# A gMLP block with one bf16 gelu per row tile, in-place batched norms, and outputs three tiles behind the gates

## The chip, the cores and the metric

The kernel runs on one core of a Trainium2 chip. The metric is device time in microseconds (us), from one launch of the whole program; a median over several executions is given, and one execution was recorded by the hardware profiler.

The engines go by these names: PE is TensorE's matmul stream and PEld its weight loads, DVE is VectorE, ACT is ScalarE, POOL is GpSimd, SP is SyncE, which here only issues DMAs. Each engine runs its own instructions in program order, and engines wait for each other by semaphores.

## The reference, cut to what matters

Rows are S = 2048 tokens of 512 features. The model alternates two mixers, twice:

```
x = x + A(layernorm(x))      # attention over segments of 32 rows with 8 memory rows, 32 heads of 128
x = x + B(layernorm(x))      # gMLP
x = x + A(layernorm(x))
x = x + B(layernorm(x))
```

Only B is changed. It is, with Fh = 688:

```
z  = gelu_tanh(x @ w_in)                       # 2048 x 1376
z1 = z[:, :688]
z2 = layernorm(z[:, 688:])                     # over the 688 features
g  = w_sp @ z2 + b_sp[:, None]                 # w_sp is 2048 x 2048: it mixes the rows
B  = (z1 * g) @ w_out                          # 688 x 512
```

Inputs and the output are bf16; x is kept in f32 in between. The layer norms have no learned scale or shift.

## The kernel before, in words

The program is a chain of four stages, A, B, A, B. In time the first B stage lies at about 781 to 939 us of the span and the second at 1697 us to the end. `a_block` (L479) is the attention; `b_block` (L227) is the gMLP and takes all of the change but two lines.

**Row tiles.** The 2048 rows are 16 tiles of 128 (NT = 16). Three arrays in device memory carry rows from stage to stage: `xd` holds x in f32, `xb_d` the normalised rows in bf16 for B, `xn_d` those for A. `o_d` holds the attention's output before x is added to it.

**Order.** Inside `b_block` the instructions of PE, DVE, ACT and SP are issued in the order in which the program text makes them (`manual_schedule`). Those of POOL are placed by a scheduler. A tile of a pool of n buffers waits for the last reader of the tile n before it; when a pool is closed, its memory goes to later pools, whose first writers wait for the last users.

**Projection half.** For each row tile `project` (L261) makes 12 matmuls (L266) into one of two PSUM tiles `big` of three banks each: tile tt + 2 can't start before ACT has emptied tile tt. The columns of w_in are swapped when they are loaded, so columns 0 to 687 of the PSUM tile are the z2 part. ACT empties it with two gelus: L268 writes the z2 part in f32 to a small tile (four buffers), L269 the z1 part in bf16 to the persistent array `z1`. DVE then takes the statistics of the f32 z2 (two bn_stats, L273 and L274, one aggregate, L275). After every second tile `norms` (L277) works out 1/sqrt(var + eps) for the pair on DVE, by a bit trick and three Newton steps (`_rstd_dve`, L119, 12 small operations), and one more operation for the shift `nb` = -mean * rstd (L285). `normalise` (L289) on ACT scales and shifts a tile into the persistent bf16 array `z2n`; it is called two tiles after the pair's statistics, so that it stands behind the gelus of the next pair in ACT's order. Transposed loads bring the normalised input rows (`front.load_rows`, on SP's queue).

**Late rows.** Four of the 16 row tiles (12 to 15) have their attention output so late that A's end doesn't add x to it. `late_load` (L253) issues the loads of x and o (L207, L208) and the add on POOL (L213), which stores x back to `xd` (L214); The calls of `norms` after tiles 5 and 7 are given two late rows each: they take the rows' statistics on DVE, and `y_norm` (L219) normalises the rows on DVE (L223) and stores them to `xb_d` on POOL's queue, from where `load_rows` reads them for the last tiles. The third and fourth late row borrow buffers of other pools, one of them a buffer of the w_sp pool.

**Gate half.** `gate(t)` makes 32 matmuls (L332) for an output row tile t: 16 source tiles `st`, each in two column halves of 344, into a PSUM tile taken from the same two `big` buffers. The weights are a transposed tile of w_sp, loaded by `load_wsp` (L257) on SP's queue into one of three buffers. `product(t)` (L335) first issues the load of w_sp tile t + 3, then forms u = (g + b_sp) * z1 on DVE (L340) in one of two u buffers, whose last 80 columns are zero, and a transposing DMA on SP's queue makes `uT`. `load_x` fetches the residual rows on ACT's queue. `finish(t)` (L357) makes six matmuls (L360), five over 128 features and one over the last 48 (`FCH`), adds x on DVE and stores the row tile on ACT's queue; in block one it also takes the statistics for the next A, with the square root by two ACT functions, and for tiles 0 and 1 normalises the rows for A's start. finish(t - 2) stands inside gate(t), after source tile 9. At the start gates 0 and 1 run through source tiles 0 to 13 first, then 14 and 15. The last tile is turned by PE (`turn_u`, L349) and copied by two ACT copies (L354, L355) in place of a DMA.

**FILL_AHEAD.** In A each segment's matmul instructions are padded, by splitting a few matmuls in two, so that a segment takes three pages of 256 PE instructions; `FILL_AHEAD` (L29, read in `pads_of`, L671) says how far the first segment of each A stage is off. The count depends on how many PE instructions come before.

Of the kernel before, what the change touches and what calls it, by code (L numbers as in the profile page):

```python
# [8 lines left out]
F32 = mybir.dt.float32  # L9
# [19 lines left out]
FILL_AHEAD = ((0, 0, 0, 106), (0, 0, 0, 94))  # L29
FCH = [(0, 128), (128, 128), (256, 128), (384, 128), (512, 128), (640, 48)]  # L30
# [137 lines left out]
class _Rows:  # L168
# [33 lines left out]
    def y_load(self, tb, first, eng, x=None, o=None):  # L202
# [5 lines left out]
        eng.dma_start(o, self.o_d[M + tb * P:M + (tb + 1) * P, :])  # L208
        self.y[tb] = (o, x)

# [8 lines left out]
    def y_norm(self, tb, mean, rstd, store):  # L219

        o, _ = self.y.pop(tb)
        xn = self.pool.tile([P, DM], BF16, name="ln_xn", bufs=2)
        self.nc.vector.tensor_scalar(out=_nat(xn[:]), in0=_perm(o), scalar1=mean, scalar2=rstd, op0=ALU.subtract, op1=ALU.mult)  # L223
        store.dma_start(self.xb_d[tb * P:(tb + 1) * P, :], xn[:])


def b_block(tc, c, rows, front, xd, MV_out, RS_out, w_sp, w_out, S, first, out_final=None):  # L227
# [4 lines left out]
    with ExitStack() as ctx:  # L232
# [5 lines left out]
        ps_pool = ctx.enter_context(tc.tile_pool(name="b_ps", bufs=1, space=PSUM))  # L238
        big = _Tagged(ps_pool, "big", 2)
        one = _Tagged(ps_pool, "one", 2)  # L240
# [3 lines left out]
        z1 = mid.tile([P, NT, FH], BF16, name="z1")  # L244
        z2n = mid.tile([P, NT, FH], BF16, name="z2n")
        w_out_sb = mid.tile([P, 6, DM], BF16, name="w_out_sb")
        xt, z2, wsp, mv, rs, nb = {}, {}, {}, {}, {}, {}
# [5 lines left out]
        def late_load(tb, x=None, o=None):  # L253
            rows.y_load(tb, first, nc.gpsimd, x=x, o=o)
            rows.y_add(tb, first, nc.gpsimd, nc.gpsimd)

        def load_wsp(t):  # L257
            wsp[t] = wsp_pool.tile([P, NT, P], BF16, name="wspT", tag="wspT")
            nc.sync.dma_start_transpose(out=wsp[t][:], in_=w_sp[t * P:(t + 1) * P, :].rearrange("t (st s) -> t st s", s=P))

        def project(tt):  # L261
# [5 lines left out]
            z2[tt] = zp.tile([P, FH], F32, name="z2", bufs=4)  # L267
            nc.scalar.activation(out=z2[tt][:], in_=pz[:, 0:FH], func=ACT.Gelu_apprx_tanh)  # L268
            nc.scalar.activation(out=z1[:, tt, :], in_=pz[:, FH:FF], func=ACT.Gelu_apprx_tanh)  # L269
            if tt % 2 == 0:  # L270
                mv[tt // 2] = zp.tile([P, 4, 2], F32, name="mv")
            st = zp.tile([P, 2, nc.vector.BN_STATS_DIM], F32, name="bnst2")
            nc.vector.bn_stats(out=st[:, 0, :], in_=z2[tt][:, 0:344])  # L273
            nc.vector.bn_stats(out=st[:, 1, :], in_=z2[tt][:, 344:FH])  # L274
            nc.vector.bn_aggr(out=mv[tt // 2][:, tt % 2, :], in_=st[:])  # L275

        def norms(q, late):  # L277

            n = 4 if late else 2
# [647 lines left out]
```

The softmax here doesn't subtract the row's maximum and nothing guards it: scores larger than these inputs give would overflow.

## Time and profile before

| | before |
|---|---|
| median of 8 runs | 1847.6 us (1842.64 to 1859.84) |
| the profiled execution | 1854.23 us |
| its span | 1852.5 us |
| PE busy | 1751.1 us, 95% of the span |
| PEld busy | 1246.1 us, 67% |
| DVE busy | 1155.2 us, 62% |
| ACT busy | 1111.2 us, 60% |
| POOL busy | 136.9 us, 7% |
| mean granted TensorE clock | 0.991 |

By stage, in the same execution (busy us in each stretch):

| stretch of the span | length | PE | DVE | ACT | POOL | clock | DMA share |
|---|---|---|---|---|---|---|---|
| first A | 781.0 | 734.1 | 508.5 | 515.9 | 57.0 | 0.99 | 0.19 |
| B one, projection half | 47.3 | 38.5 | 37.6 | 32.6 | 15.0 | 1.00 | 0.61 |
| B one, gate half | 110.7 | 102.8 | 44.7 | 14.4 | 11.9 | 0.97 | 0.80 |
| second A | 758.0 | 736.5 | 495.8 | 510.8 | 37.6 | 0.99 | 0.16 |
| B two, projection half | 46.1 | 37.8 | 37.4 | 31.8 | 15.1 | 1.00 | 0.66 |
| B two, gate half | 109.4 | 101.4 | 31.1 | 5.7 | 0.3 | 0.98 | 0.67 |

How to read it: busy time counts an engine's own instructions; DMA issues and waits don't count as busy. Matmuls are pipelined and their ends are modelled, so a busy PE is not PE at its peak. The clock is the share of full TensorE speed that the chip granted. The DMA share is the mean busy share of the core's 16 DMA engines. The lines "A <- B" in a view of waits say that A's engine stood idle until B's instruction or DMA had finished.

The chain of work that ended last is PE for 86% of the span, DVE 4, DMA 4, issue 2, ACT 2, POOL 1. Of that, the gate matmuls (L332) are 7%, the output matmuls (L360) 3%, the projection's (L266) 1% of the span and the transposed u tiles 1%; most of the rest is attention.

### The profile page before, as it was taken

The page shows a single profiled execution, that of the slowest core. Times are in us where ns is not written, and L with a number is a line of the kernel's source. Part 1 is how long each engine was busy: PE and PEld are TensorE (multiplying, and loading weights), DVE is VectorE, ACT ScalarE, POOL GpSimd, SP SyncE. Part 2 cuts the span into 40 slices and gives each one's busy share as a digit, 9 for nine tenths or more (in the row PEclk, how much of TensorE's full clock was granted, in tenths as well). Part 3 has the DMA queues.
Part 4 walks back from the last instruction along what each step waited for, and adds up shares of the span by engine and source line. Part 5 has one row for each costly group of instructions (what it writes and reads, how often), then busy time and mean ns, then how long its engine had stood idle before and what let it go on. Part 6 is the DMA issues. An engine that isn't in the chain of part 4 may idle for free.

```text
span 1852.5 us, 109472 instructions
## 1 busy us (share of the span) xinstructions
PE 1751.1 (95%) x51176; PEld 1246.1 (67%) x51176; DVE 1155.2 (62%) x2700; ACT 1111.2 (60%) x2074; POOL 136.9 (7%) x289
## 2 busy tenths in 40 slices
PE   2999999999999999889989999999999999998798
PEld 1777777777777777645557777777777777775455
DVE  1666666677667766583346666666766676665722
ACT  1677777776667776471047667666776676665500
POOL 5000000000000000122010000000000000002000
PEclk8999999999999999999989999999999999999999
DMA  9100000021002111359830000001200120124585
GB/s 348 53 20 19 22 20 20 20 82 31 19 20 84 37 30 42 92 140 201 185 120 22 23 23 24 22 22 43 82 26 22 50 83 26 35 62 144 119 174 131
DMA packets 189327, 126.78 MB, mean 68 GB/s; under 512 B 135896, under 2 KB 164328, under 8 KB 188872
## 3 DMA queue, kind: packets, MB, share of 16 engines
q1 hardware_dynamic: 167016, 71.01, 16.4%
q0 software_dynamic: 10560, 34.07, 5.6%
q10 hardware_dynamic: 11296, 14.70, 2.6%
q8 instruction: 400, 6.55, 1.5%
q14 instruction: 55, 0.45, 0.1%
HBM read 59.29 MB, written 33.56 MB: 50 GB/s over the span
## 4 chain that ended last, share of the span: by engine, by line
PE 86%; DVE 4%; DMA 4%; issue 2%; ACT 2%; POOL 1%; SPq 0%; ACTq 0%; POOLq 0%; DVEq 0%
PE psm L544 24%; PE psV L544 13%; PE pw L599 12%; PE psb L544 10%; PE pg L332 7%; PE psS L722 5%; PE psO L745 4%; PE pwB L611 3%; PE py L360 3%; PE psD L797 2%; PE psM L787 1%; DMA uT<-u 1%; PE pz L266 1%; DMA Wo_sb<-in_A_Wo_dram 1%; PE psM L788 1%
## 5 line engine op out<-in xcount | busy, mean ns | idle before, releaser
L544 PEld LDWEIGHTS <-hA 128*32 128x32 bf16 x19868 | 541.8, 96 | 168.7 <-DVE hA L655 51.5
L701 ACT CAST rows<-psm 128x512 bf16<-128x512 f32 x512 | 300.1, 586 | 200.0 <-PE psm L544 200.0
L544 PE MATMUL psm<-Wq_sb,hA 128*32 128x256 bf16 (+1 forms) x5768 | 275.9, 319 | 10.9 <-DVE hA L655 9.5
L599 PE MATMUL pw<-Wo_sb,uT 128*32 128x128 bf16 x16640 | 264.3, 220 | 17.3 <-DVE uT L807 9.3
L599 PEld LDWEIGHTS <-uT 128*32 128x32 bf16 x16640 | 236.7, 97 | 63.6 <-DVE uT L807 50.5
L544 PE MATMUL psm<-Wk_sb,hA 128*32 128x256 bf16 (+1 forms) x6623 | 276.4, 298 | 1.8 <-issue 1.0
L544 PE MATMUL psV<-Wv_sb,hA 128*32 128x256 bf16 x7477 | 274.1, 284 | 0.9 <-issue 0.9
L705 DVE STREAM_TRANSPOSE QQ<-rows 128x512 bf16<-128x512 bf16 x256 | 182.0, 711 | 78.3 <-ACT rows L701 77.2
L726 ACT ACTIVATE E<-psS 128x448 bf16<-128x448 f32 x256 | 140.0, 547 | 121.6 <-PE psS L722 121.6
L757 DVE TENSOR_TENSOR uT<-psO,Rt 128x384 bf16<-128x384 f32 x256 | 138.6, 541 | 119.2 <-ACT Rt L813 118.9
L705 DVE STREAM_TRANSPOSE KA<-rows 128x512 bf16<-128x512 bf16 x256 | 181.8, 710 | 44.5 <-ACT rows L701 44.3
L807 DVE TENSOR_TENSOR uT<-psO,Rm 128x128 bf16<-128x128 f32 x256 | 62.6, 287 | 167.7 <-PE psD L797 167.7
L813 ACT ACTIVATE Rt<-Rt 128x512 f32<-128x512 f32 x256 | 157.4, 629 | 4.1
L332 PE MATMUL pg<-z2n,wspT 128*128 128x344 bf16 x1024 | 155.6, 310 | 1.0 <-DVE u L340 1.0
L332 PEld LDWEIGHTS <-wspT 128*128 128x128 bf16 x1024 | 98.2, 98 | 55.0 <-issue 8.2
L805 ACT ACTIVATE Rt<-psD 128x1024 f32<-128x1024 f32 x128 | 131.2, 1025 | 6.0
L544 PEld LDWEIGHTS <-hB 128*32 128x32 bf16 x3072 | 88.1, 97 | 68.0 <-DVE hB L559 24.9
L722 PEld LDWEIGHTS <-KA 128*64 128x64 bf16 x2048 | 79.8, 113 | 67.1 <-DVE KA L705 40.2
L729 DVE TENSOR_TENSOR E<-E,maskN 128x448 bf16<-128x448 bf16 x256 | 95.3, 372 | 45.4 <-ACT E L726 45.4
L544 PE MATMUL psb<-Wq_sb,hB 128*32 128x512 bf16 x1024 | 91.6, 389 | 25.9 <-DVE hB L559 25.9
L782 ACT CAST VA<-psV 128x512 bf16<-128x512 f32 x128 | 75.0, 586 | 61.9 <-PE psV L544 61.9
L722 PE MATMUL psS<-QQ,KA 128*64 128x80 bf16 x2048 | 110.1, 208 | 1.9 <-issue 1.0
(147 smaller groups left out, 2219.3 us busy)
## 6 DMA issues: line engine op xcount, KB each, us to landing
Wo_sb<-in_A_Wo_dram POOLq DMA_DIRECT2D x8, 1024.0 KB, 13.2
xs<-xd ACTq DMA_DIRECT2D x32, 256.0 KB
o_d<-o_sb SPq DMA_DIRECT2D x126, 64.0 KB
y_o<-o_d SPq DMA_DIRECT2D x24, 256.0 KB
xd<-y_o SPq DMA_DIRECT2D x22, 256.0 KB
Wq_sb<-in_A_Wq_dram POOLq DMA_DIRECT2D x8, 512.0 KB, 6.9
Wk_sb<-in_A_Wk_dram POOLq DMA_DIRECT2D x8, 512.0 KB, 10.9
Wv_sb<-in_A_Wv_dram POOLq DMA_DIRECT2D x8, 512.0 KB, 11.4
```

The lines of the kernel that those rows point to most:

```text
L332: nc.tensor.matmul(pg[t][:, k, 0:344], lhsT=wsp[t][:, st, :], rhs=z2n[:, st, 344 * k:344 * k + 344], start=(st == 0), stop=(st == NT - 1))
L544: nc.tensor.matmul(o, lhsT=lhs(kt, cg), rhs=r, start=(kt == 0 and a == 0), stop=(kt == KT - 1 or halved > 0), tile_position=(0, 32 * cg), ...
L599: nc.tensor.matmul(po[32 * cg:32 * cg + 32, 0:128], lhsT=lhs[:, n, :], rhs=wo_rhs(h, cg), start=(h == 0), stop=(h == H - 1), tile_position ...
L701: nc.scalar.copy(r[:], ps[:])
L705: nc.vector.transpose(out=QQ[:, j % 2, :, 0:32] if j < 2 else KA[:, j % 2], in_=r[:])
L722: nc.tensor.matmul(pS[64 * g:64 * g + 64, i, c0:80 if K is KA else 112], lhsT=K[:, r, n:n + 2, :].rearrange("p h k -> p (h k)"), rhs=q if ...
L726: nc.scalar.activation(out=E[:, r], in_=pS, func=ACT.Exp, scale=scale)
L729: nc.vector.tensor_tensor(out=E[:, r], in0=E[:, r], in1=maskN[:, j4, :].unsqueeze(1).to_broadcast([P, 4, 112]), op=ALU.mult)
L757: nc.vector.tensor_tensor(out=hview(uT_nxt[:], r, 8, 32), in0=oview(r, 8, 32), in1=Rr[:, :, :, 0:24], op=ALU.mult)
L782: nc.scalar.copy(VA[:, 1].rearrange("p i e -> p (i e)"), psV[1][:, 0, :])
L805: nc.scalar.activation(out=Rt[:], in_=psD[:], func=ACT.Ln)
L813: nc.scalar.activation(out=rt, in_=rt, func=ACT.Exp, scale=-1.0)
```

## The change

Nearly all of it lies in `b_block`; what is computed stays the same, but for roundings.

- **One z tile, one gelu.** `z1` and `z2n` become the two halves of one bf16 array `z` (16 x 1376 columns per partition), and one gelu over 1376 columns writes it. The f32 z2 tiles go, and the statistics are taken from the bf16 values.
- **Norms in place, in four batches.** The scalars are worked out for groups instead of pairs: row tiles 0 to 3 with two late rows, 4 to 6 with the other two, 7 to 11, and 12 to 15. `normalise` overwrites z2 in `z`; on ACT, after the gelus as the loop says, and for the last four tiles on DVE.
- **Late rows.** All eight loads are issued first, each x and then (by the function that `y_load` now returns) its o, in the order of the four late rows; then a memset and the loads of w_out, which came before them. The adds move from POOL to DVE (`late_sum`), after tile 3 and after tile 5, and the normalising moves from DVE to ACT (`late_norm`).
- **w_sp loads** start after tiles 2, 4 and 11 (7, 9 and 11 before).
- **PSUM.** The projection keeps two tiles of three banks, in a pool that ends with it; the gates get three tiles of two banks.
- **Padded last rows.** w_out's sixth block is zeroed first, so that all six output matmuls and all six transposes are over 128 rows and one ACT copy replaces two. `FCH` goes.
- **Three tiles behind.** uT gets three buffers, gates 0 and 1 stop first at source tile 11, gate 2 runs whole, and finish(t - 3) stands inside gate(t). After the last gate come finish(13), the turn of tile 15, finish(14), finish(15). `load_x(t - 1)` stands in `product(t)`, behind the transpose.
- **FILL_AHEAD** of the second A: 94 becomes 86.

A's own use of `y_load` calls the returned function at once. In the diff, `NT - 4 + k` is the late row's tile. The core of the diff:

```diff
-FILL_AHEAD = ((0, 0, 0, 106), (0, 0, 0, 94))
-FCH = [(0, 128), (128, 128), (256, 128), (384, 128), (512, 128), (640, 48)]
+FILL_AHEAD = ((0, 0, 0, 106), (0, 0, 0, 86))
...
-        eng.dma_start(o, self.o_d[M + tb * P:M + (tb + 1) * P, :])
         self.y[tb] = (o, x)
+        return lambda: eng.dma_start(o, self.o_d[M + tb * P:M + (tb + 1) * P, :])
...
-    def y_norm(self, tb, mean, rstd, store):
+    def y_norm(self, tb, mean, rstd, store, shift=None):
 
         o, _ = self.y.pop(tb)
         xn = self.pool.tile([P, DM], BF16, name="ln_xn", bufs=2)
-        self.nc.vector.tensor_scalar(out=_nat(xn[:]), in0=_perm(o), scalar1=mean, scalar2=rstd, op0=ALU.subtract, op1=ALU.mult)
+        if shift is not None:
+            self.nc.scalar.activation(out=_nat(xn[:]), in_=_perm(o), func=ACT.Identity, bias=shift, scale=rstd)
+        else:
+            self.nc.vector.tensor_scalar(out=_nat(xn[:]), in0=_perm(o), scalar1=mean, scalar2=rstd, op0=ALU.subtract, op1=ALU.mult)
         store.dma_start(self.xb_d[tb * P:(tb + 1) * P, :], xn[:])
...
-        ps_pool = ctx.enter_context(tc.tile_pool(name="b_ps", bufs=1, space=PSUM))
-        big = _Tagged(ps_pool, "big", 2)
-        one = _Tagged(ps_pool, "one", 2)
+        big = _Tagged(zctx.enter_context(tc.tile_pool(name="b_psz", bufs=1, space=PSUM)), "big", 2)
...
-        z1 = mid.tile([P, NT, FH], BF16, name="z1")
-        z2n = mid.tile([P, NT, FH], BF16, name="z2n")
+        z = mid.tile([P, NT, FF], BF16, name="z")
+        z2n, z1 = z[:, :, 0:FH], z[:, :, FH:FF]
...
-        def late_load(tb, x=None, o=None):
-            rows.y_load(tb, first, nc.gpsimd, x=x, o=o)
-            rows.y_add(tb, first, nc.gpsimd, nc.gpsimd)
...
-            z2[tt] = zp.tile([P, FH], F32, name="z2", bufs=4)
-            nc.scalar.activation(out=z2[tt][:], in_=pz[:, 0:FH], func=ACT.Gelu_apprx_tanh)
-            nc.scalar.activation(out=z1[:, tt, :], in_=pz[:, FH:FF], func=ACT.Gelu_apprx_tanh)
-            if tt % 2 == 0:
-                mv[tt // 2] = zp.tile([P, 4, 2], F32, name="mv")
+            nc.scalar.activation(out=z[:, tt, :], in_=pz[:, 0:FF], func=ACT.Gelu_apprx_tanh)
             st = zp.tile([P, 2, nc.vector.BN_STATS_DIM], F32, name="bnst2")
-            nc.vector.bn_stats(out=st[:, 0, :], in_=z2[tt][:, 0:344])
-            nc.vector.bn_stats(out=st[:, 1, :], in_=z2[tt][:, 344:FH])
-            nc.vector.bn_aggr(out=mv[tt // 2][:, tt % 2, :], in_=st[:])
-
-        def norms(q, late):
-
-            n = 4 if late else 2
-            for k, tb in enumerate(late):
-                rows.y_stats(tb, mv[q][:, 2 + k, :])
-            rs[q] = zp.tile([P, 4], F32, name="rs")
-            nb[q] = zp.tile([P, 2], F32, name="nb")
-            _rstd_dve(nc, zp, rs[q][:, 0:n], mv[q][:, 0:n, 1], n)
-            nc.vector.scalar_tensor_tensor(out=nb[q][:], in0=mv[q][:, 0:2, 0], scalar=-1.0, in1=rs[q][:, 0:2], op0=ALU.mult, op1=ALU.mult)
-            for k, tb in enumerate(late):
-                rows.y_norm(tb, mv[q][:, 2 + k, 0:1], rs[q][:, 2 + k:3 + k], nc.gpsimd)
-
-        def normalise(tt):
-            nc.scalar.activation(out=z2n[:, tt, :], in_=z2.pop(tt)[:], func=ACT.Identity, bias=nb[tt // 2][:, tt % 2:tt % 2 + 1],
-                                 scale=rs[tt // 2][:, tt % 2:tt % 2 + 1])
-
+            for k in range(2):
+                nc.vector.bn_stats(out=st[:, k, :], in_=z[:, tt, 344 * k:344 * k + 344])
+            nc.vector.bn_aggr(out=slot(tt), in_=st[:])
+
+        def slot(tt):
+            group = next(g for g in GROUPS if tt in g)
+            if group not in where:
+                where[group] = (zp.tile([P, 8, 2], F32, name="mv"), zp.tile([P, 8], F32, name="rs"), zp.tile([P, 8], F32, name="nb"))
+            return where[group][0][:, group.index(tt), :]
+
+        def norms(group):
+
+            mv, rs, nb = where[group]
+            n = len(group)
+            _rstd_dve(nc, zp, rs[:, 0:n], mv[:, 0:n, 1], n)
+            nc.vector.scalar_tensor_tensor(out=nb[:, 0:n], in0=mv[:, 0:n, 0], scalar=-1.0, in1=rs[:, 0:n], op0=ALU.mult, op1=ALU.mult)
+
+        def scalars(tt):
+            group = next(g for g in GROUPS if tt in g)
+            k = group.index(tt)
+            mv, rs, nb = where[group]
+            return mv[:, k, 0:1], rs[:, k:k + 1], nb[:, k:k + 1]
+
+        def normalise(*tts, dve=False):
+            for tt in tts:
+                mean, rstd, shift = scalars(tt)
+                if dve:
+                    nc.vector.tensor_scalar(out=z2n[:, tt, :], in0=z2n[:, tt, :], scalar1=mean, scalar2=rstd, op0=ALU.subtract, op1=ALU.mult)
+                else:
+                    nc.scalar.activation(out=z2n[:, tt, :], in_=z2n[:, tt, :], func=ACT.Identity, bias=shift, scale=rstd)
+
+        def late_sum(k):
+            rows.y_add(NT - 4 + k, first, nc.vector, nc.gpsimd)
+            rows.y_stats(NT - 4 + k, slot(("row", k)))
+
+        def late_norm(k):
+            mean, rstd, shift = scalars(("row", k))
+            rows.y_norm(NT - 4 + k, mean, rstd, nc.gpsimd, shift=shift)
+
+        GROUPS = ((0, 1, 2, 3, ("row", 0), ("row", 1)), (4, 5, 6, ("row", 2), ("row", 3)), (7, 8, 9, 10, 11), (12, 13, 14, 15))
+        wl = wsp_pool.tile([P, 2, DM], F32, name="wspL", tag="wspT")
+        places = ((None, None), (gp.tile([P, DM], F32, name="xs", bufs=3)[:], gp.tile([P, DM], F32, name="xo", bufs=1)[:]),
+                  tuple(gp.tile([P, DM], F32, name="xs", bufs=3)[:] for _ in range(2)), (wl[:, 0, :], wl[:, 1, :]))
+        for load in [rows.y_load(NT - 4 + k, first, nc.gpsimd, *places[k]) for k in range(4)]:
+            load()
+        nc.gpsimd.memset(w_out_sb[:, 5, :], 0.0)
         nc.gpsimd.dma_start(w_out_sb[:, 0:5, :], w_out[0:640, :].rearrange("(fc p) d -> p fc d", p=P))
         nc.gpsimd.dma_start(w_out_sb[0:48, 5, :], w_out[640:688, :])
-        late_load(NT - 4)
-        late_load(NT - 3, gp.tile([P, DM], F32, name="xs", bufs=3)[:], gp.tile([P, DM], F32, name="xo", bufs=1)[:])
-        late_load(NT - 2, *(gp.tile([P, DM], F32, name="xs", bufs=3)[:] for _ in range(2)))
-        wl = wsp_pool.tile([P, 2, DM], F32, name="wspL", tag="wspT")
-        late_load(NT - 1, wl[:, 0, :], wl[:, 1, :])
         for tt in range(NT):
             project(tt)
-            if tt in (7, 9, 11):
-                load_wsp((tt - 7) // 2)
-            if tt == 14:
-                load_x(0)
-            if tt % 2 == 1:
-                if tt // 2 + 3 < NT // 2:
-                    front.load_rows(tt // 2 + 3)
-                norms(tt // 2, {5: (NT - 4, NT - 3), 7: (NT - 2, NT - 1)}.get(tt, ()))
-                if tt > 1:
-                    normalise(tt - 3)
-                    normalise(tt - 2)
-        normalise(NT - 2)
-        normalise(NT - 1)
+            if tt % 2 == 1 and tt // 2 + 3 < NT // 2:
+                front.load_rows(tt // 2 + 3)
+            if tt in (2, 4, 11):
+                load_wsp((2, 4, 11).index(tt))
+            if tt == 3:
+                late_sum(0)
+                late_sum(1)
+                norms(GROUPS[0])
+                late_norm(0)
+                late_norm(1)
+                normalise(0)
+            elif tt == 4:
+                normalise(1)
+            elif tt == 5:
+                late_sum(2)
+                late_sum(3)
+                normalise(2)
+            elif tt == 6:
+                norms(GROUPS[1])
+                late_norm(2)
+                late_norm(3)
+                normalise(3)
+            elif tt in (7, 8, 9):
+                normalise(tt - 3)
+            elif tt == 11:
+                norms(GROUPS[2])
+                normalise(7)
+            elif tt in (12, 13):
+                normalise(2 * tt - 16, 2 * tt - 15)
+        norms(GROUPS[3])
+        normalise(12, 13, 14, 15, dve=True)
 
...
+        ps_pool = ctx.enter_context(tc.tile_pool(name="b_psg", bufs=1, space=PSUM))
+        two = _Tagged(ps_pool, "two", 3)
+        one = _Tagged(ps_pool, "one", 2)
...
-                pg[t] = big.tile([P, 3, 512], F32, name="pg")
+                pg[t] = two.tile([P, 2, 512], F32, name="pg")
...
+            uT[t] = up.tile([P, 6, P], BF16, name="uT", bufs=3)
             if t + 1 < NT:
-                load_x(t + 1)
-
-                uT[t] = up.tile([P, 6, P], BF16, name="uT")
                 nc.sync.dma_start_transpose(out=uT[t][:], in_=u[t][:].rearrange("t (fc s) -> t fc s", s=P))
+            if t > 0:
+                load_x(t - 1)
 
         def turn_u(t):
             pT = one.tile([P, 1024], BF16, name="pT")
-            for fc, (f0, fsz) in enumerate(FCH):
-                nc.tensor.transpose(pT[0:fsz, fc * P:(fc + 1) * P], u[t][:, f0:f0 + fsz], ident_bf[:])
-            uT[t] = up.tile([P, 6, P], BF16, name="uT")
-            nc.scalar.copy(uT[t][:, 0:5, :].rearrange("p fc r -> p (fc r)"), pT[:, 0:640])
-            nc.scalar.copy(uT[t][0:48, 5, :], pT[0:48, 640:768])
+            for fc in range(6):
+                nc.tensor.transpose(pT[:, fc * P:(fc + 1) * P], u[t][:, fc * P:(fc + 1) * P], ident_bf[:])
+            nc.scalar.copy(uT[t][:].rearrange("p fc r -> p (fc r)"), pT[:, 0:768])
 
         def finish(t):
             py = one.tile([P, DM], F32, name="py")
-            for fc, (f0, fsz) in enumerate(FCH):
-                nc.tensor.matmul(py[:], lhsT=uT[t][0:fsz, fc, :], rhs=w_out_sb[0:fsz, fc, :], start=(fc == 0), stop=(fc == 5))
+            for fc in range(6):
+                nc.tensor.matmul(py[:], lhsT=uT[t][:, fc, :], rhs=w_out_sb[:, fc, :], start=(fc == 0), stop=(fc == 5))
...
-        gate(0, range(0, NT - 2))
-        gate(1, range(0, NT - 2))
-        gate(0, range(NT - 2, NT))
+        gate(0, range(0, NT - 4))
+        gate(1, range(0, NT - 4))
+        gate(0, range(NT - 4, NT))
         product(0)
-        gate(1, range(NT - 2, NT))
+        gate(1, range(NT - 4, NT))
         product(1)
-        for t in range(2, NT):
+        gate(2, range(0, NT))
+        product(2)
+        for t in range(3, NT):
             gate(t, range(0, 10))
-            finish(t - 2)
+            finish(t - 3)
             gate(t, range(10, NT))
             product(t)
+        load_x(NT - 1)
+        finish(NT - 3)
+        turn_u(NT - 1)
         finish(NT - 2)
-        turn_u(NT - 1)
         finish(NT - 1)
```

## The prediction, made before the changed kernel was run

> **What bounds the kernel now.** I read four views. The row of engine shares says TensorE is busy 95% of the span, so only what makes TensorE wait or slow down is worth time. The edit touches the two gMLP blocks, so I next read TensorE's waits inside the first (781 to 939 us of the span):
>
> ```profile
> PE pz L266 <- ACT z L269: 8.2, 5, 2.5
> PE py L360 <- DMA uT<-u: 4.8, 3, 2.5
> PE py L360 <- ACT uT L354: 2.3, 1, 2.3
> PE pg L332 <- DVE u L340: 0.5, 1, 0.5
> ```
>
> (engine, line, releaser: us in total, times, longest). In the second block the same four read 8.3, 2.6, 1.4 and 0.5. So the projection half loses 8 us to ScalarE handing back PSUM, and the gate half 7.6 and 4.5 us, mostly to transposed u tiles. The windows view shows the load of the stretches:
>
> ```profile
> 781.00:828.00 47.00, 38.16 (x193) 18.65 (x191) 37.40 (x138) 32.36 (x46) 15.04 (x23) 1.00 0.60 152
> ...
> 846.00:932.00 86.00, 83.72 (x510) 48.69 (x510) 35.23 (x58) 6.84 (x28) 11.40 (x18) 0.99 0.91 193
> ```
>
> (stretch, length, busy us of PE, PEld, DVE, ACT, POOL, TensorE clock, DMA share, GB/s). In the projection VectorE is busy 37.4 us beside TensorE's 38.2: two near-equal bounds. In the gate loop only TensorE is full, with the DMA engines at 0.91 behind it. Last the timeline, for how the waits arise:
>
> ```profile
> 804.57 4.81 PE L266 MATMUL pz<-front 128*128 128x512 bf16 x24 [2.48 <-ACT z L269]
> ...
> 807.80 1.81 ACT L290 ACTIVATE z2n<-z,nb,rs 128x688 bf16<-128x688 f32 x2 [2.02 <-DVE nb L285]
> ```
>
> ```profile
> 843.88 2.73 PE L360 MATMUL py<-w_out_sb,uT 128*128 128x512 bf16 x6 [2.49 <-DMA uT<-u]
> ...
> 865.17 0.09 PEld L360 LDWEIGHTS <-uT 48*128 48x128 bf16 x1 [0.42 <-issue]
> ```
>
> A normalise waits 2 us for VectorE's scalars; the gelu queued behind it is late, so is the PSUM bank. The six output matmuls at 843.88 take 2.73 us where 1.56 is usual, right after a wait. The 48-row weight load starts only after 0.42 us of idling, which no 128-row load shows.
>
> [...] the gelus stand behind the waiting normalise. [...] 2.3 to 2.9 us of idling was followed by slow matmuls (2.73 for 1.56, then the next 32 gates 5.26 for 4.84), some 1.6 us lost each time; in the projection gaps of 2.5 us cost nothing. [...] The trace has 735 to 739 ns for 688 elements and 954 with two pointers[...].
>
> **The change, part by part.** Times below count from the first projection matmul of block one (782.17); before, the gates begin at 46.1 (828.31).
>
> *One gelu for two.* 1.24 us of ScalarE per tile where two starts of 0.63 took 1.26: nothing. Each gelu starts 2.52 after its tile's first matmul, as the first of the two did (782.17 to 784.69), since that waited for the whole tile too. PSUM comes free 1.33 later, before 1.37: nothing.
>
> *First gelu.* z is now one tile, on memory that yB occupied, so the first gelu must wait for the store of yB, and in the changed program the table load stands behind that wait. Before, only the second gelu waited (787.19). New: 787.19 + table load 1.28 = 6.30 for gelu 0, so tile 2 starts at 6.30 + 1.33 + 0.06 = 7.69 (before 5.82). TensorE waits 3.0.
>
> *Four batches in place, late rows on VectorE.* Removed: four of the eight chains of 13 small VectorE operations (2.42 us each, 827.25 to 829.67), the four POOL adds (1.16 each) and what they did to VectorE (one 0.16 operation took 2.86 at 797.18). Added on VectorE: four adds of 0.69 (row L213 DVE), so a late row is add, statistics, aggregate, 0.73 + 0.72 + 0.19 = 1.64. The price is order. Before, ScalarE waited for scalars begun two tiles earlier; now it waits, with the next gelu behind it, for a batch that contains the tile just finished:
> Tile 3: gelu 3 runs 12.54 to 13.87. VectorE: 0.05 + statistics 1.09 + two late rows 3.28 + chain 2.42, to 20.71. ScalarE: two late norms 1.44, one normalise 0.90, then gelu 4 from 23.10 to 24.43, tile 6 at 24.49. Tiles 4 and 5 covered TensorE to 17.01: it waits 7.5.
> Tile 6: gelu 5 starts at 25.24, VectorE ends tile 5 at 27.7, rows 2 and 3 at 31.0, tile 6 and chain at 34.5; ScalarE 1.44 + 0.90, gelu 7 from 36.9 to 38.2, tile 9 at 38.28. TensorE was through at 33.2: 5.1.
> Tile 11: gelu 11 ends at 48.5, scalars 52.05, normalise 7, gelu 12 to 54.3, tile 14 at 54.39 for 51.6: 2.8. Then two normalises stand before gelu 13: 0.7.
> After each of the two long waits [...] 1.7 lost: the first is hidden by VectorE's queue, the second passes through (counted above).
>
> *Gates.* Their PSUM pool replaces the projection's, and the first gate now waits for gelu 15 (before for gelu 14): 60.32 + 1.33 + 0.06 = 61.7, a wait of 2.0. In sum 16 tiles of 2.33, 3.4 of slow clock, waits 3.0 + 7.5 + 5.1 + 2.8 + 0.7 + 2.0: 61.8 against 46.1, so +15.6 in block one; +15.9 in block two, where the store of yB lands 0.5 later. The last four norms on VectorE (0.34 to 0.78 each) are done 64.9 + 3.1 = 68.3 at the latest; the gates need them at 61.7 + 48 × 0.1463 = 68.7: hidden, barely. With TensorE at 40% over the last 9 us I take the gates to start on the slow clock: 1.7 per block.
>
> *Padded rows.* The weight load of the sixth output matmul no longer stands alone: finish takes 1.49 (864.00 to 865.49) and five loads are 0.20 apart, so 1.29 is left: 0.2 × 16 per block. The memset (POOL) has 50 us to spare.
>
> *Three tiles behind, three u tiles and PSUM pairs.* Gates 0 to 2 run through, 96 × 0.1463 = 14.05. Then 13 periods of 4.68 + 1.29 = 5.97, 77.6. The tail of block one: finish 1.29, transposes 0.5, finish 1.29, a wait of 1.4 for the copy behind the rstd of tile 13, finish 1.35: 5.9, sum 97.6 against 110.4 (828.31 to 938.73). Block two, no rstd: 4.45, sum 96.1 against 105.8. Gain 12.8 + 9.7 = 22.5. The next stage's first matmuls ran slow before (1.90 and 1.81 for 1.05); with 1.4 idle in place of 2.3 they should not: 1.6 more (0 to 2.6). The third weight tile is asked for 5.9 us before use, and such loads took about 4.4 to 6.4 from the start of issue: minus 0.3 per block. Gain 23.5. Loads of x come one period later, still a period and a half ahead; u buffers are rewritten two periods on, past their transpose.
>
> *FILL_AHEAD.* 94 to 86 splits four more matmuls: it makes up for nine fewer TensorE instructions before (51187 to 51178), so the next stage stands where it did. Nothing.
>
> Net: 15.6 + 15.9 + 3.4 − 23.5 = +11.4 us. The profiled execution took 1854.23 (span 1852.5) and would take 1865.6; its median over eight runs is 1847.6, so 1859. A measurement here tells about 0.5%, 9.2 us, from no change.
>
> **Rivals.** *The clock stays up* (not slower): the projection showed no slow matmuls after 2.5 us gaps. It takes away 3.4 + 3.4: +4.6, 1852. It decides if slow tiles cost under 4.6 us in all. Against it: waits of 5 and 7 us are longer than any now.
> *The gate loop stays at its old pace*: DMA share 0.91 in block one; if transposes still hold finish, or hold the u buffer that product rewrites, the 0.2 per tile (3.2) and the two late stalls (2.7) stay, and slow clock after the 3.0 and 2.8 waits adds up to 1.7 each per block: 1865 to 1872.
> *ScalarE lets the gelu pass* (faster): were gelus 4, 7 and 12 not held by the norms before them, the waits 7.5, 5.1, 2.8 and 3.4 of clock per block would go: −37, 1822. It decides once waits fall by half. Against: first-in-first-out, and L354 now stands behind an rstd in just that way. A smaller kin: bf16 statistics at double rate would save 0.4 per chain, some 3 us.
>
> **How the numbers follow.** Worked sum 0.40 (1854 to 1864); clock stays 0.25 (1848 to 1856); slower gates or clock 0.26 (1863 to 1874); gelu passes or waits otherwise hidden 0.09. Slower by over 0.5% is above 1856.8: 0.7 of the first and all of the third, 0.54. Faster 0.09, the rest 0.37. The range leaves out the last case and the edges of the others: 1845 to 1873.
>
> **What would show it.** The changed profile should have TensorE waiting for the gelu's release about 19 us per block in place of 8.2, longest 7; ScalarE waiting some 7, 4 and 3.5 us for nb; gates starting 61 to 62 us after the first projection matmul; a 5.97 us gate period; no uT waits. It is wrong if the late norms are not behind VectorE's chain, if statistics on bf16 take half the 0.43 us, or if the period stays at 6.17.

## The result and the profile after

The changed kernel took 1867.1 us in the median of its runs (1857.5 to 1871.8), where the kernel before took 1848.9 us in the runs made beside them. The ratio of the means is 1.0085, with a 95% interval of 1.0068 to 1.0103. On the 1847.6 us that were shown before, this is about 1863 us: slower by 15.7 us, 12.6 to 19.0. The forecast was 1859 us and slower.

Executions of one kernel differ by several us in the attention stages alone, as the runs below show, so the two traces are compared stage by stage. "Projection" runs from the first projection matmul to the first gate matmul, "gates" from there to the end of the last output matmul, "attention two" from there to the next projection, "end" from the last output matmul to the end of the execution. All are differences of starts and ends in the timeline, in us.

| profiled execution | projection 1 | gates 1 | attention two | projection 2 | gates 2 | end | whole |
|---|---|---|---|---|---|---|---|
| before | 46.1 | 110.4 | 758.2 | 46.3 | 105.8 | 5.3 | 1854.2 |
| before, again | 45.8 | 108.9 | 745.7 | 45.9 | 106.1 | 5.3 | 1837.8 |
| changed | 63.7 | 97.4 | 749.4 | 61.6 | 96.5 | 6.8 | 1856.8 |
| changed, again | 61.9 | 99.2 | 755.3 | 63.7 | 96.5 | 6.8 | 1867.8 |

So the gMLP pays about 17 us per block in its projection half and gets 10 us back per block in its gates. The windows of the same stretches in the changed kernel's first profile (stretch, length, busy us of PE, PEld, DVE, ACT, POOL, TensorE clock, DMA share, GB/s):

```profile
781.30:844.97 63.67, 44.75 (x192) 20.59 (x192) 29.70 (x98) 35.17 (x36) 10.68 (x20) 0.87 0.50 112
844.97:942.38 97.41, 96.22 (x614) 59.63 (x613) 43.30 (x82) 8.91 (x30) 11.45 (x20) 1.00 0.94 193
```

VectorE's busy time fell, from 37.4 to 29.7 us, and ScalarE's rose only from 32.4 to 35.2, yet the half became 17 us longer: no engine has too much work, they wait for each other. TensorE's waits over the first block say for whom:

```profile
PE pz L264 <- ACT z L265: 17.5, 4, 7.1
PE pg L368 <- ACT z L265: 1.4, 1, 1.4
PE py L394 <- ACT uT L389: 0.7, 1, 0.7
```

The wait for the gelu (L265; before L269) went from 8.2 us in five pieces of at most 2.5 to 17.5 us in four pieces of up to 7.1. The wait for a transposed u tile, 4.8 us before, is gone. ScalarE's own waits in block two show what the gelu stood behind:

```profile
ACT ln_xn L223 <- DVE nb L282: 11.5, 2, 6.8
...
ACT L265 <- DMA o_d<-yB: 4.7, 1, 4.7
ACT z L296 <- DVE nb L282: 3.8, 1, 3.8
```

Two late norms waited 6.8 and 4.7 us for VectorE's scalars, one normalise 3.8 us, and the table load ahead of the first gelu 4.7 us for the store of yB. These are the four waits of the forecast. In ScalarE's timeline of block one (start, length, and in brackets the idle time ahead):

```profile
795.65 1.32 ACT L265 ACTIVATE z<-pz 128x1376 bf16<-128x1376 f32 x1 [1.67 <-PE pz L264]
803.77 0.81 ACT L223 ACTIVATE ln_xn<-y_o,nb,rs 128x512 bf16<-128x512 f32 x1 [6.80 <-DMA xd<-y_o]
804.49 0.80 ACT L223 ACTIVATE ln_xn<-xo,nb,rs 128x512 bf16<-128x512 f32 x1
805.19 0.94 ACT L296 ACTIVATE z<-z,nb,rs 128x688 bf16<-128x688 bf16 x1
806.04 1.29 ACT L265 ACTIVATE z<-pz 128x1376 bf16<-128x1376 f32 x1
```

Gelu 3 ends at 796.97; gelu 4 starts at 806.04. The matmuls of tiles 4 and 5 were done by 800.3. The bracket names a DMA, but VectorE's last operation for the scalars (L282) ran from 803.57 to 803.74, and that is what ended the wait. The two PSUM tiles cover 4.7 us of such a delay; the rest is TensorE's wait of 7.1.

The gates in the timeline, to be read against the period of 6.17 us before:

```profile
861.89 1.46 PE L394 MATMUL py<-w_out_sb,uT 128*128 128x512 bf16 x6
863.18 4.83 PE L368 MATMUL pg<-z,wspT 128*128 128x344 bf16 x32
867.85 1.46 PE L394 MATMUL py<-w_out_sb,uT 128*128 128x512 bf16 x6
```

From one finish to the next it is 5.96 us, without a wait.

### The profile page after: what moved, and what is told of

The parts are those of the page before. It is cut to its first block, busy times and chain, and to the rows that moved or that the text cites. A ratio compares the mean times of both kernels' runs of the same rounds, so it can differ in the third digit from the quotient of the medians.

```text
span 1855.0 us, 109315 instructions
## 1 busy us (share of the span) xinstructions
PE 1743.5 (94%) x51180; PEld 1246.8 (67%) x51180; DVE 1137.6 (61%) x2604; ACT 1107.7 (60%) x2040; POOL 128.2 (7%) x283
## 4 chain that ended last, share of the span: by engine, by line
PE 87%; DMA 4%; DVE 3%; ACT 3%; issue 2%; POOL 1%; POOLq 0%; DVEq 0%; ACTq 0%
PE psm L582 24%; PE psV L582 13%; PE pw L637 12%; PE psb L582 9%; PE pg L368 8%; PE psS L760 5%; PE psO L783 4%; PE pwB L649 4%; PE psD L835 2%; PE py L394 2%; PE pz L264 2%; PE psM L825 1%; DMA Wo_sb<-in_A_Wo_dram 1%; ACT z L265 1%; PE psM L826 1%
## 5 line engine op out<-in xcount | busy, mean ns | idle before, releaser
L368 PE MATMUL pg<-z,wspT 128*128 128x344 bf16 x1024 | 153.9, 309 | 2.8 <-ACT z L265 2.8
L368 PEld LDWEIGHTS <-wspT 128*128 128x128 bf16 x1024 | 100.1, 98 | 56.0 <-issue 3.2
L767 DVE TENSOR_TENSOR E<-E,maskN 128x448 bf16<-128x448 bf16 x256 | 95.2, 372 | 44.3 <-ACT E L764 44.3
```

Source lines behind the costliest of these rows:

```text
L368: nc.tensor.matmul(pg[t][:, k, 0:344], lhsT=wsp[t][:, st, :], rhs=z2n[:, st, 344 * k:344 * k + 344], start=(st == 0), stop=(st == NT - 1))
L767: nc.vector.tensor_tensor(out=E[:, r], in0=E[:, r], in1=maskN[:, j4, :].unsqueeze(1).to_broadcast([P, 4, 112]), op=ALU.mult)
```

## The experiments

Theory: the loss is one of order. A norm that waits for VectorE's scalars stands ahead of the next gelu on ScalarE, for longer than two PSUM tiles cover; to this comes the first gelu's wait for the store of yB. The gate half is a gain of its own. Rivals: that the gates gain less than one profile shows, that VectorE is the bound, that the clock makes the loss, that the late norms' ScalarE time does. The runs were made on several chips, on which the median of the kernel before is 1839 to 1853 us. So each ratio below is to runs of the kernel before on the same chip, and runs on different chips are compared by their ratios or by their stages.

### The old projection with the new gates

```diff
   (b_block before, with the changed code from zctx.close() on,)
-        if tt == 14: load_x(0)
+        nc.gpsimd.memset(w_out_sb[:, 5, :], 0.0)
```

> The projection half of the kernel before (pair norms, f32 z2, late rows on POOL) with the changed gate half (padded rows, three tiles behind, PSUM pool of its own). Theory: the loss of the change lies wholly in its projection half and the gate half gains 13 + 9.3 us, so this runs 18 to 22 us below the kernel before (about 1828), with gate stages of 97 us and projection stages of 46 to 48. Rival: the gate half gains little over several executions, because its clock or its DMAs vary (the profiled execution was a lucky one): then within 10 us of the kernel before.

Measured: ratio 0.9920 to the kernel before (0.9892 to 0.9947), some 15 us less. Projections 48.4 and 48.8 us, gates 97.4 and 96.5. The gate half's stages came out as expected. With the old projection the loss of 17 us per block shrinks to 2.5 and 2.7 us against the means of before, 1.5 us of it a wait of the first gate for the last gelu. The total fell short of the expected 18 us by these and by 2.7 us at the two ends (the last experiment).

### Norms three gelus later

```diff
-            if tt == 3: ... late_norm(0); late_norm(1); normalise(0)     (and so on, each norm in its batch's tile)
+            (late_norm on DVE, behind norms(GROUPS[0]) and norms(GROUPS[1]))
+            if 6 <= tt < 15:
+                normalise(tt - 6)
+            if tt == 15:
+                normalise(9, 10, 11)
```

> The changed kernel, but each ACT normalise stands three gelus later than its batch's statistics (normalise(tt - 6) behind gelu tt), and the late rows are normalised on DVE right behind the batch's scalars, as before the change. Same operations otherwise. Theory (gelus held behind norms that wait for DVE): the waits of 7.1, 4.7 and 2.7 us and the slow clock after them go, the gates start about 43.6 us after the first projection matmul in place of 62 to 64, so 35 to 39 us per run below the changed kernel (about 1829). Rival (DVE is the bound, with the late rows' adds moved to it): the stage stays above 52 us, 20 us below at most.

Measured: ratio 0.9892 (0.9864 to 0.9920). Projections of 44.3 and 44.9 us, where 43.6 was expected. TensorE's waits in the first block and the stage behind it:

```profile
PE pz L264 <- ACT z L265: 3.6, 2, 2.2
PE psb L576 <- DVE xo L397: 2.2, 1, 2.2
PE pg L362 <- DMA wspT<-in_B_w_sp_dram: 2.1, 1, 2.1
```

The 17.5 us are down to 3.6 with the operations all still there, and VectorE, which was the rival's bound, does the same work and the four late norms besides in a half of 44 us. The order is what cost, with a share for the late norms that the next run measures. Gates 1 became 101.4 us: in the middle of the loop one w_sp tile is late by 2.1 us, and the 20 gate matmuls behind it take 4.77 us where 3.08 is usual. I took it for the third tile, loaded behind tile 11, when I put the parts together below; the timeline has it at 875 us, at the start of gate 9, and the third tile is that of gate 2.

### Late norms alone back on DVE

```diff
-            rows.y_norm(NT - 4 + k, mean, rstd, nc.gpsimd, shift=shift)
+            rows.y_norm(NT - 4 + k, mean, rstd, nc.gpsimd)
```

> The changed kernel, but the late rows are normalised on DVE behind the batch's scalars, as before the change; the normalise calls keep their places. Theory (what costs is that a norm which waits for DVE's scalars stands ahead of the next gelu): ACT is free 1.44 us earlier after batches one and two, so the waits of tiles 6 and 9 shrink by about that and the projection half ends some 3 us earlier, at 58 to 61 us. Rival (the late norms on ACT are what costs): it falls to about 45 us, as in the run with the norms later.

Measured in one execution: projections of 56.4 and 56.2 us, some 6 us less than changed, between theory and rival and lower than the 58 expected. TensorE's wait for the gelu in block one (17.5 us in the changed kernel):

```profile
PE pz L264 <- ACT z L265: 11.3, 4, 5.8
```

The first wait shrank from 7.1 to 5.8 us, as two late norms of 0.7 us each are worth. The second, 4.7 us at tile 9, went but for 0.25 us at tile 10 (1.07 in block two): the gelus of tiles 4 and 5, and so VectorE's second batch, came earlier as well, and I had counted each wait by itself. The other 11 to 12 us per block between this and the run above are the place of the normalise calls, the only edit in which the two runs differ.

### z of the first two tiles on other memory

```diff
+        zap = ctx.enter_context(tc.tile_pool(name="b_za", bufs=1))     (opened just ahead of the b_z pool)
-        z = mid.tile([P, NT, FF], BF16, name="z")
+        za = zap.tile([P, 2, FF], BF16, name="za")
+        zb = mid.tile([P, NT - 2, FF], BF16, name="z")
```

> The changed kernel, but z of row tiles 0 and 1 lies in a small tile of its own on memory that A's last DMAs don't read, so that the first gelu and the table load need not wait for the store of yB. Theory: the 3.0 us wait of tile 2 and the slow clock behind it (1.7) go, and everything behind moves up: 4.7 us per block, 9 in all. Rival: the late rows' loads arrive no earlier, so DVE's adds behind tile 3 absorb what is won: 0 to 4 us in all, with a longer wait at tile 6.

Measured: ratio 1.0026 (1.0015 to 1.0037), that is 10.9 us below the changed kernel's ratio; projections 58.4 and 58.6, some 4.2 us less each. The expected 9 us are there (8.4 by the stages): tile 2 no longer waits, and the longest wait stays at 7.1 us, so the rival's longer wait at tile 6 did not come.

### Idle matmuls in the waits

```diff
+            if not first and tt in (2, 6, 9, 14):
+                fill_wait(tt, {2: 11, 6: 30, 9: 19, 14: 11}[tt])      (matmuls into a spare PSUM bank)
             pz = big.tile([P, 1536], F32, name="pz")
```

> The changed kernel with idle matmuls, in block two alone, into a spare PSUM bank whose result nobody reads: 11, 30, 19 and 11 of them ahead of tiles 2, 6, 9 and 14, where TensorE waits for ACT. Theory (each wait of 2.7 us or more is followed by about 1.7 us lost to a slow clock): in block two the mean clock of the projection half goes from 0.89 to about 1, the tiles behind the waits take 2.3 us, and gates start some 4 to 7 us earlier than 61.6 after the first projection matmul, with the same waits of ACT for nb. Rival (the slow stretch only fills time that DVE's chain sets): the clock goes up, and the gates start within 1 us of 61.6.

Measured in one execution: in block two the mean clock rose to 0.97, and the gates still started at 60.96 us, against 61.6 and 63.7 in the two profiles of the changed kernel. TensorE's timeline of block two:

```profile
1709.89 7.13 PE L274 MATMUL pz<-front 128*128 128x512 bf16 x36 [0.66 <-ACT z L275]
1716.86 4.26 PE L265 MATMUL pfill<-front 128*128 128x512 bf16 x19
1723.40 3.94 PE L274 MATMUL pz<-front 128*128 128x512 bf16 x12 [2.28 <-ACT z L275]
```

Tiles 6 to 8 now take 2.3 us each, but tile 9 waits 2.28 us more behind its fillers: what the clock gives is waited away again. Of the 4 to 7 us that my theory of the clock expected, 0.7 to 2.7 came, by which of the two profiles one compares with. The rival's forecast, within 1 us of 61.6, came true in this one execution.

### The padded rows alone

```diff
-FCH = [(0, 128), ..., (640, 48)]
+FCH = [(128 * i, 128) for i in range(6)]
+        nc.gpsimd.memset(w_out_sb[:, 5, :], 0.0)
```

> The kernel before with only the sixth block of w_out and the last output matmul padded to 128 rows. Theory: the 48-row weight load costs 0.2 us per row tile, so the gate period goes from 6.17 to 5.97, each gate stage loses 3.2 us, the kernel 6.4 (ratio 0.9965). Rival (the DMA of uT sets the period): the wait for uT grows by what is saved, ratio 1.

Measured: ratio 0.9989 (0.9975 to 1.0002). The timeline has the expected period of 5.96 us where nothing waits. TensorE's wait for uT in block one went to 5.8 us in five pieces (4.8 in three, and 4.2 in two, in the two profiles of before):

```profile
PE py L360 <- DMA uT<-u: 5.8, 5, 2.6
```

Gates 1 lost only 1 to 3 us, while gates 2 lost 4.5. So it looks as if the transposes take back a part of the saving in block one when finish is only two tiles behind. Whether and how much, one profile and an interval that reaches 1 don't settle. No run has finish three tiles behind without the padding, so how the gates' gain divides between the two is open as well.

### The kernels before and after, profiled again

> The kernel before once more, for a second profiled execution. Its first one had 758 us between the end of the first gMLP and the start of the second, where the four changed kernels profiled since had 746 to 749. Theory (that stage varies from execution to execution by stalls that have nothing to do with the change): about 746 to 750 us here, with projection stages of 46 us and gate stages of 110 and 106. Rival (the change makes the second attention stage shorter): 755 us or more again.

Attention two took 745.7 us: the 758 of the first profile was that execution's, not the kernel's.

> The changed kernel once more, for a second profiled execution on this chip. Theory: projection halves of 61 to 64 us, gate stages of 97 and 96, and 745 to 749 us between the two gMLPs, so a span some 12 to 15 us above that of the kernel before. Rival (a typical execution of the changed kernel loses more, in the gates or in attention, than the first profile shows): a gate stage of 100 us or more, or 753 us or more between the gMLPs.

The projections and gates 2 came as expected; gates 1 took 99.2 us with three waits for w_sp, 1.3 us together. Attention two took 755.3 us, which is the rival's number. Over all the profiles this stage lies between 745 and 758 us for kernels of both kinds, with single segments of up to 5 us more than the usual 11.3; I don't read a difference out of it.

### Putting the parts together

```diff
   (norms three gelus later, late norms on DVE, z of tiles 0 and 1 apart)
-            if tt in (2, 4, 11):
-                load_wsp((2, 4, 11).index(tt))
+            if tt in (2, 4, 9):
+                load_wsp((2, 4, 9).index(tt))
-            xo = gp.tile([P, DM], F32, name="xo", bufs=1)
+            xo = gp.tile([P, DM], F32, name="xo", bufs=2)
```

> The changed kernel with four edits: norms three gelus later and late norms on DVE, z of tiles 0 and 1 in a tile of its own, the third w_sp load behind tile 9 in place of 11, and two xo buffers in place of one. Theory: projection halves of 41 to 42 us, gate stages of 97 us without the wait for w_sp, the first attention matmul about 1.1 us behind the last output matmul in place of 2.3, and 5.3 us from the last matmul to the end in place of 6.8. About 45 us below the changed kernel, a ratio of 0.983 to 0.986 to the kernel before. Rival: the projection stays at 44 us because DVE's late rows then hold batch two, ratio 0.988.

Measured: ratio 0.9887 (0.9857 to 0.9916), the rival's number for another reason. Projection 1 took the expected 41.0 us, projection 2 took 52.9, and TensorE's waits of block two named a load:

```profile
PE pz L272 <- DMA front<-xb_d: 11.3, 1, 11.3
```

SP's queue in the same block (start, time in which SP was held by the issue):

```profile
1674.16 5.28 SPq L263 DMA_TRANSPOSE wspT<-in_B_w_sp_dram  x1
1679.53 5.57 SPq L163 DMA_TRANSPOSE front<-xb_d  x1
1685.15 11.68 SPq L263 DMA_TRANSPOSE wspT<-in_B_w_sp_dram  x1
```

The rows of tile 8 were asked for at 1679.5, right behind one w_sp tile, and were there only at 1697.9. The changed kernel, with its slower projection, shows no wait for rows. Gates 1 still took 100.1 us, with 2.2 us of waits for w_sp tiles in the middle of the loop: moving the third load did not take them away.

```diff
-            if tt in (2, 4, 9):
-                load_wsp((2, 4, 9).index(tt))
+            if tt in (7, 8, 9):
+                load_wsp(tt - 7)
```

> The kernel of the run with four edits (norms three gelus later, z of tiles 0 and 1 apart, two xo buffers), but the three first w_sp loads stand behind tiles 7, 8 and 9 in place of 2, 4 and 9, so that none stands on SP's queue ahead of the normalised rows of tiles 8 and 10. Theory (tile 8 waited 11.3 us for rows whose load was issued between two w_sp loads): that wait goes, projection halves of 41 to 42 us in both blocks, a ratio of 0.983 to 0.986 to the kernel before. Rival (the rows were late for another reason, such as the loads of w_out): a wait of several us for rows stays in one block or the other, ratio 0.988 or above.

Measured: ratio 0.9883 (0.9848 to 0.9917); projections 44.4 and 46.8 us. Tile 8's wait is gone. A wait for rows of 4.0 us in block one and 5.9 in block two stands at tile 14 now:

```profile
PE pz L272 <- DMA front<-xb_d: 4.0, 1, 4.0
...
PE pz L272 <- DMA front<-xb_d: 5.9, 1, 5.9
```

Its rows are the late ones, which VectorE hands on in its second batch, at 810 us of the span in block one, and they are stored and loaded again before tile 14 can start. So the theory held for the wait that it named and not for the time, which is the rival's.

```diff
-        GROUPS = ((0, 1, 2, 3, ("row", 0), ("row", 1)), (4, 5, 6, ("row", 2), ("row", 3)), ...
+        GROUPS = ((0, 1, 2, 3, ("row", 0), ("row", 1), ("row", 2), ("row", 3)), (4, 5, 6), ...
```

(with all four late_sum and late_norm behind tile 3)

> The kernel of the run before (norms later, z of tiles 0 and 1 apart, w_sp loads behind tiles 7 to 9, two xo buffers), with all four late rows summed behind tile 3 and taken into the first batch of scalars, in place of two there and two behind tile 5. Theory (tile 14 waited 4.0 and 5.9 us for rows that DVE's second batch handed on at 810 us): the wait goes, projection halves of 41 to 42 us in both blocks, gates not slowed, a ratio of 0.982 to 0.985 to the kernel before. Rival (the loads of the third and fourth late row, or the two ln_xn buffers, hold DVE so long that batch one is late for gelu 6): a wait of ACT for nb of 2 us or more appears at tile 6, halves of 44 us or more.

Measured: ratio 0.9832 (0.9799 to 0.9865), 31 us below the kernel before and lower than the two runs above, though the intervals overlap. Projections 43.3 and 42.3 us, gates 97.5 and 96.5, end 5.3. TensorE's waits in block one:

```profile
PE pz L272 <- ACT z L273: 2.2, 1, 2.2
...
PE pz L272 <- DMA front<-xb_d: 0.3, 1, 0.3
```

Theory and rival both had a share: the wait for rows is down from 4.0 to 0.3 us, and a wait of ScalarE for batch one (3.3 us in its own waits) makes one of 2.2 us, as the rival said.

### Two xo buffers alone

```diff
-            xo = gp.tile([P, DM], F32, name="xo", bufs=1)
+            xo = gp.tile([P, DM], F32, name="xo", bufs=2)
```

> The changed kernel with two xo buffers in place of one, and nothing else. Theory (at the end finish(13), (14) and (15) follow each other so closely that each addition waits for the store of the one before, which has the only buffer): the first attention matmul of the second stage comes 1.1 us behind the last output matmul in place of 2.3, and the execution ends 5.3 us behind the last matmul in place of 6.8; projection and gate halves as before. Rival (the order of the turn and the finishes causes it): both stay at 2.3 and 6.8.

Measured in one execution: 1.1 and 5.3 us, as the theory said. The last additions in VectorE's timeline of the changed kernel:

```profile
1846.41 0.69 DVE L399 TENSOR_TENSOR xo<-py,xs 128x512 bf16<-128x512 f32 x1 [0.36 <-PE py L394]
1848.96 0.69 DVE L399 TENSOR_TENSOR xo<-py,xs 128x512 bf16<-128x512 f32 x1 [1.85 <-DMA out_dram<-xo]
1851.50 0.69 DVE L399 TENSOR_TENSOR xo<-py,xs 128x512 bf16<-128x512 f32 x1 [1.85 <-DMA out_dram<-xo]
```

and with two buffers:

```profile
1850.73 0.69 DVE L399 TENSOR_TENSOR xo<-py,xs 128x512 bf16<-128x512 f32 x1 [1.54 <-PE py L394]
1852.03 0.69 DVE L399 TENSOR_TENSOR xo<-py,xs 128x512 bf16<-128x512 f32 x1 [0.60 <-PE py L394]
```

Before the change, the turn of tile 15 lay between the last two finishes, and their additions, 3.5 us apart, waited for TensorE and not for the store:

```profile
1849.00 0.69 DVE L365 TENSOR_TENSOR xo<-py,xs 128x512 bf16<-128x512 f32 x1 [2.85 <-PE py L360]
```

## Why the prediction came out as it did

The direction, the range and the mechanism of the loss were right. The sum was +11.4 us; by stages, with the means of the two profiles of each kernel, it is +13.6: projections +33.4, gates -20.8, ends +1.0. The timed runs say +15.7, with 13.6 inside their interval. That the sums lie 2.2 us apart is partly luck: the parts missed by +1.9 (projections), -3.4 (gates on a slow clock), +1.1 (gates) and +2.6 (ends), and these nearly cancel.

**Projection half: +31.5 forecast, +33.4 measured.** The times from the first projection matmul, of the first profile:

| | forecast | block one | block two |
|---|---|---|---|
| tile 2 starts | 7.7 | 7.8 | 7.7 |
| tile 6 starts | 24.5 | 26.1 | 24.3 |
| tile 9 starts | 38.3 | 39.6 | 37.8 |
| tile 14 starts | 54.4 | 55.8 | 53.7 |
| gates start | 61.8 | 63.7 | 61.6 |

Block two follows the forecast within 0.7 us. Block one is late from tile 6 on, by 1.3 to 1.9 us: its tiles 2 and 3 ran slow behind the 3.0 us wait (6.49 us for 24 matmuls in place of 4.81), which I had excluded since waits of 2.5 us had cost nothing. In block two the same wait of 2.9 us had no such effect, and in the run with the norms later one of 2.2 us had. The two places in TensorE's timeline of the changed kernel:

```profile
789.12 6.49 PE L264 MATMUL pz<-front 128*128 128x512 bf16 x24 [3.00 <-ACT z L265]
...
1699.53 4.81 PE L264 MATMUL pz<-front 128*128 128x512 bf16 x24 [2.92 <-ACT z L265]
```

Tiles 14 and 15 ran slow too in this profile (6.49 us in both blocks, behind a wait of 2.7), which the forecast doesn't have; shorter waits behind them, 1.4 us in place of 0.7 and 2.0, gave most of it back. The lengths that the forecast gives ScalarE's new operations are my estimates, and the first profile bears them out: 1.31 us for the gelu (1.33), the next start 1.20 behind its own (1.24), and 0.81 for a late norm (0.80). Before, ScalarE took 0.59 us for 512 values (L885) and 0.74 for 688 (L268); the same 0.15 us for 176 values leads to 1.32 for 1376 and, from the 0.95 of a normalise of 688 (L290), to 0.80 for a late norm of 512. A normalise in place took 0.95, as the row of before has it.

**Slow clock.** The tiles behind the two long waits were slow, as forecast: in block one 36 matmuls took 8.85 us behind the 7.1 us wait, where they take 7.13 behind the idle matmuls, and 12 took 4.17 behind the 4.7 us wait, where they take 2.48. The granted clock was 0.50 over 807.39:810.80, behind the first of these waits, and 1.00 over 811:816. The 1.7 us that the forecast puts on each wait is an estimate of mine; 1.7 it was twice in block one, and 1.3 and 1.4 in block two (8.46 and 3.89 us). That only about one of these two losses makes the half longer is in line with the idle matmuls, which won 0.7 to 2.7 us. The step that failed is the 1.7 us per block for gates that start slow, which I had assumed: the first gates of block one ran at full speed, 0.147 us per matmul at a granted clock of 1.00, in spite of the 1.4 us wait ahead and the thin projection before.

```profile
844.97 15.33 PE L368 MATMUL pg<-z,wspT 128*128 128x344 bf16 x104 [1.40 <-ACT z L265]
```

**Gates: -21.9 without that term, -20.8 measured.** Period 5.97 forecast and 5.96 measured; gates 2 96.1 and 96.5. The padding was rightly sized per tile; the run with the padding alone hints that with finish two tiles behind the transposes take part of it back. The third weight tile that I allowed 0.3 us cost nothing in one profile; in the second the waits for w_sp, later in the loop, made 1.3.

**Ends: -1.6 forecast, +1.0 measured.** Beside the slow gates this is the largest miss. The next stage's first matmuls did get their clock back in both profiles (the first four groups took 3.8 us, where the two of before have 5.0 and 5.8; in the first profile of each, the granted clock was 1.00 over 944.65:948.40 and, before, 0.51 over 939.83:943.10). But the runs don't tie this to the change: with the same changed ending they took 5.1 us again in three runs (old projection, norms later, idle matmuls), and with the old ending and the padding alone 3.5. What I left out: the three finishes in a row share one xo buffer, so each addition waits for a store, 1.1 us at the end of block one and 1.55 at the end of the program. The forecast counted TensorE's tail and not what is queued behind the single buffer.

**Rivals.** "The gelu passes" is refuted by ScalarE's timeline. Moving the norms shows what it would have been worth: 37 us were given for the case, and the run with norms later lies by its stages 36.1 us in the projections below the changed kernel's first profile. "The clock stays up" came true for the gates, and in the projection it would have won little, as the idle matmuls show. "The gate loop stays at its old pace" did not happen, though its range from 1865 on holds the raw median: right size, wrong cause. The smaller kin of the gelu's rival, statistics at double rate on bf16 values, did not come either: 0.51 us for 344 values, 0.50 before.

## What to carry to other kernels

Batching small operations saved time (with four chains of them gone, VectorE's busy time fell from 37.4 to 29.7 us here) but moved the moment of the result to the end of the batch. What counts on an engine that runs its operations in order, as ScalarE does in these timelines, is whether the result is there when its user reaches the head of the queue, and how many buffers cover the delay: here gelu 4 started 9 us behind the end of gelu 3, against two PSUM tiles, 4.7 us. Calling the users three tiles later, with the late norms back on VectorE, kept the batches and turned a loss of 0.85% into a gain of 1.1%, and 1.7% once the other waits (a first tile on memory still being stored, loads queued behind large ones, rows handed on late, one store buffer at the end) were taken out in turn.

## What the runs showed of the hardware that was not expected

The clock after a wait doesn't follow the wait's length alone. At tile 2, waits of 2.2 and 3.0 us were followed by slow tiles (6.49 us for 24 matmuls) and one of 2.9 us was not (4.81); within the second profile of the changed kernel one of 2.77 us was not (block one, 4.81 us) and one of 2.79 was (block two, 6.45 us). In the old projection a wait of 2.5 us cost nothing before the change, and with the new gates 24 matmuls behind one of 2.5 us took 6.49 us in block one, in place of 4.81. What decides it is open. And rows asked for right behind a large transposed load can come late: in the run with four edits they were there 18 us after the request, and SP was held for 5 to 12 us by a single issue of a w_sp load; with the w_sp loads moved behind them this wait was gone.
